# One product for mask and shift, the maxima masked on VectorE, whole-block key copies by two engines in turn: a decode attention kernel on Trainium2

## The chip, the cores and the metric

The kernel runs on one core of a Trainium2 chip. The metric is device microseconds of one execution, the median of several runs. A core has TensorE (matrix products, PE in the profile, its weight loads PEld), VectorE (DVE), ScalarE (ACT), GpSimd (POOL) and SyncE (SP), which issues most of the loads here. Each engine works through its own instructions in their order, and semaphores order the engines among each other.

## The reference

Eight sequences, one new token each, 32 query heads over 8 key heads of width 128, and the last 1024 positions of a cache of 4096. The attention output is gated by a feed-forward network (GEGLU, inner width 1792) of the same normalised input.

```python
def _A_ref(x, k_cache, v_cache, wq, wo):
    W = min(4096, max(256, Sk // 4))
    rep = Hq // Hkv
    q = (x @ wq).reshape(B, Sq, Hq, Dh).transpose(0, 2, 1, 3)
    k = jnp.repeat(k_cache[:, :, Sk - W:, :], rep, axis=1)
    v = jnp.repeat(v_cache[:, :, Sk - W:, :], rep, axis=1)
    scores = jnp.einsum("bhqd,bhkd->bhqk", q, k) * (Dh ** -0.5)
    p = _softmax(scores, axis=-1)
    o = jnp.einsum("bhqk,bhkd->bhqd", p, v)
    return o.transpose(0, 2, 1, 3).reshape(B, Sq, Hq * Dh) @ wo
...
x = A_x
xn = _layernorm(x, axis=-1)
s = _A_ref(xn, A_k_cache, A_v_cache, A_wq, A_wo)
g = _silu((_gelu(xn @ B_w_gate) * (xn @ B_w_up)) @ B_w_down)
return x + s * g
```

## The kernel before

The order of all work is written out by hand: each engine executes in program order. All large loads are issued by SyncE in one queue, into a ring of 16 buffers of 1 MB: first the feed-forward weights, then wq, then key and value blocks in turn, with half a megabyte of wo after every second value block. In all 47.5 MB are read.

At the start TensorE runs fillers (`keep_busy`, line 235: products of ones, 512 columns wide, whose result nobody reads), the layernorm's result is transposed (line 260), and the feed-forward products (lines 274 and 313) and the query products (line 349) follow, with more fillers between them.

The attention is cut into 16 sets (`q`, NQ = 16). A set is one key head and four of the eight sequences (QG = 4); a key block of a set is 4 x 1024 positions. A set has four groups (`g`, `i` = 0 to 3), one 1024-position block each. The positions lie on partitions so that a partition belongs to one of the four sequences, `partition % 4`. The 16 query columns of a set (QC: four sequences, four heads each) are multiplied with every position, so three quarters of the scores belong to the wrong sequence and are masked with -1e30.

- `transposes(g)`: eight TensorE transposes of 128x128 into one PSUM tile `kT_ps` (two such tiles); VectorE copies columns 0 to 639 into `kTa` (line 375), ScalarE the other 384 into `kTb` (line 377).
- `scores(g)`: in the first group of a set, one product of 4 rows (line 386) writes the mask over the whole score tile of 512 columns, and the eight products of line 397 add the scores on it.
- `max_keys(q)`: VectorE's maximum over the columns, per partition (line 408). `max_all(q)`: a TensorE transpose of the maxima (416), VectorE's negated maximum (418), and two diagonal matrices `diag` that hold it in a coarse and a fine part (423, 426), at rows 0 and 32.
- `exponentials(q)`: one product of ones with those rows (line 437, 48 rows) adds the shift to the score tile, then ScalarE's exponential (446) gives `pT`.
- `sums(q)`: eight products of ones with 64 columns of `pT` (451), then VectorE's sum and reciprocal (459, 465).
- `values(g)`: eight products with the value block (476). Each is 64 columns wide (VC = 4 times 16), though only the first 16 accumulate what is used; where fewer than four blocks of columns are left it is 16 wide.
- `normalise(q)` (487), and `project(h)` (502), the product with wo, two heads at a time in the second half of every other set.

The values run two sets behind the scores (LAG = 2). One step of the loop at lines 513 to 535 is, in this order: the transposes of the next group, `max_all` of the set before (step 1), the scores of this group, the sums (step 0) and values of two sets before, the exponentials of the set before (step 2), projections; at the end of a set `normalise`, then `max_keys`. At the end of the program come the last four heads' projections, the gate (541), four transposes (544), the residual (546) and the store.

Of the kernel before, what the change touches and what calls it, by code (L numbers as in the profile page):

```python
# [9 lines left out]
ALU = mybir.AluOpType  # L10
AX = mybir.AxisListType
BF16 = mybir.dt.bfloat16
FP32 = mybir.dt.float32
# [4 lines left out]
def kernel(  # L18
# [33 lines left out]
    nc = tc.nc  # L52
# [6 lines left out]
    W = min(4096, max(256, Sk // 4))  # L59
    win0 = Sk - W  # L60
    F = B_w_gate.shape[1]
    P = nc.NUM_PARTITIONS
    NDC = D // P
    NFC = F // P
    NSC = W // P
# [4 lines left out]
    QG = 4  # L70
    NB = QG
    NCS = QG * NSC
    VC = 4
    AC = 3
    NRING = 16
    MASK = -1.0e30
    NG = Hkv * B
    NQ = NG // QG
    QC = QG * rep
    SH = B // QG  # L80
    LAG = 2

    consts = ctx.enter_context(tc.tile_pool(name="consts", bufs=1))
# [4 lines left out]
    kT_pool = ctx.enter_context(tc.tile_pool(name="kT_pool", bufs=3))  # L88
    p_pool = ctx.enter_context(tc.tile_pool(name="p_pool", bufs=4))
    small = ctx.enter_context(tc.tile_pool(name="small", bufs=2))  # L90
    ps_misc = ctx.enter_context(tc.tile_pool(name="ps_misc", bufs=1, space=PSUM))
# [3 lines left out]
    ps_sum = ctx.enter_context(tc.tile_pool(name="ps_sum", bufs=1, space=PSUM))  # L95
    ps_o = ctx.enter_context(tc.tile_pool(name="ps_o", bufs=1, space=PSUM))
# [75 lines left out]
    for q in range(NQ):  # L172
# [12 lines left out]
        out=ident,  # L185
        in_=ident,
# [8 lines left out]
    ones_pp = consts.tile([P, P], BF16, name="ones_pp")  # L195
    nc.vector.memset(ones_pp, 1.0)

    row_of = consts.tile([QG, P // QG, QG], BF16, name="row_of")
    nc.vector.memset(row_of, 0.0)
    nc.gpsimd.affine_select(  # L200
        out=row_of,
        in_=row_of,
# [6 lines left out]
    other = consts.tile([QG, QG, rep], BF16, name="other")  # L209
    nc.vector.memset(other, MASK)  # L210
    nc.gpsimd.affine_select(
        out=other,
        in_=other,
# [4 lines left out]
        channel_multiplier=-1,  # L218
    )

    LO = 32
    diag = []
    for i in range(2):
        t = consts.tile([LO + QC, QC], BF16, name=f"diag{i}")
        nc.vector.memset(t, 0.0)
        diag.append(t)
    eps_sb = consts.tile([B, 1], FP32, name="eps_sb")
    nc.vector.memset(eps_sb, 1e-5)

# [3 lines left out]
    def keep_busy(n):  # L233
# [12 lines left out]
        out=rstd, in_=mv[:, 1:2], func=ACT.Sqrt, bias=eps_sb, scale=1.0  # L246
# [4 lines left out]
        out=xhat,  # L251
        in0=x_sb,
# [94 lines left out]
    for k in range(NDC):  # L347
        for m in range(Hq):
# [4 lines left out]
                start=(k == 0 and m == 0),  # L353
                stop=(k == NDC - 1),
                skip_group_check=True,
# [5 lines left out]
    kT, sc, pT, mxs, shift, recip = {}, {}, {}, {}, {}, {}  # L361

    def transposes(g):
        q, i = divmod(g, NB)
        kT_ps = ps_kT.tile([P, W], BF16, name="kT_ps")
        for c in range(NSC):
            n = i * NSC + c
            nc.tensor.transpose(  # L368
                kT_ps[:, c * P : (c + 1) * P],
                k_sb[q][:, n * Dh : (n + 1) * Dh],  # L370
                ident,
            )
        own = (NSC - AC) * P
        ta = kT_pool.tile([P, own], BF16, name="kTa")
        nc.vector.tensor_copy(out=ta, in_=kT_ps[:, 0:own])  # L375
        tb = kT_pool.tile([P, W - own], BF16, name="kTb")
        nc.scalar.copy(out=tb, in_=kT_ps[:, own:])  # L377
        kT[g] = [ta[:, c * P : (c + 1) * P] for c in range(NSC - AC)]
        kT[g] += [tb[:, c * P : (c + 1) * P] for c in range(AC)]

    def scores(g):
        q, i = divmod(g, NB)
        hkv, b = divmod(q * QG, B)
        if i == 0:
            sc[q] = ps_sc.tile([P, NCS, QC], FP32, name="sc_ps")
            nc.tensor.matmul(  # L386
                sc[q],
                row_of.rearrange("g e s -> g (e s)"),
                other.rearrange("g s j -> g (s j)")
                .unsqueeze(1)  # L390
                .to_broadcast([QG, NCS, QC]),
                start=True,
                stop=False,
                skip_group_check=True,
            )
        for c in range(NSC):
            nc.tensor.matmul(  # L397
                sc[q][:, i * NSC + c, :],
                kT[g][c],
                qT_all[:, b : b + QG, hkv * rep : (hkv + 1) * rep],  # L400
                start=False,
                stop=False,
                skip_group_check=True,
            )

    def max_keys(q):
        mx = small.tile([P, QC], FP32, name="mx")
        nc.vector.tensor_reduce(  # L408
            out=mx, in_=sc[q].rearrange("p c n -> p n c"), axis=AX.X, op=ALU.max
        )  # L410
        mxs[q] = mx

    def max_all(q):

        mxT_ps = ps_mx.tile([QC, P], FP32, name="mxT_ps")
        nc.tensor.transpose(mxT_ps, mxs[q], ident_f)
        nm = small.tile([QC, 1], FP32, name="nm")
        nc.vector.tensor_reduce(
            out=nm, in_=mxT_ps, axis=AX.X, op=ALU.max, negate=True
        )  # L420
        eye = ident_f[0:QC, 0:QC]
        parts = diag[q % 2]
        nc.vector.tensor_scalar(
            out=parts[0:QC, :], in0=eye, scalar1=nm[:, 0:1], scalar2=None, op0=ALU.mult
        )
        nc.vector.scalar_tensor_tensor(  # L426
            out=parts[LO : LO + QC, :],
            in0=eye,
            scalar=nm[:, 0:1],
            in1=parts[0:QC, :],  # L430
            op0=ALU.mult,
            op1=ALU.subtract,
        )
        shift[q] = parts

    def exponentials(q):
        nc.tensor.matmul(  # L437
            sc[q],
            ones_pp[0 : LO + QC, :],
            shift[q].unsqueeze(1).to_broadcast([LO + QC, NCS, QC]),  # L440
            start=False,
            stop=True,
            skip_group_check=True,
        )
        pT[q] = p_pool.tile([P, NCS, QC], BF16, name="pT")
        nc.scalar.activation(out=pT[q], in_=sc[q], func=ACT.Exp, scale=inv_sqrt_dh)  # L446

    def sums(q):
        sums_ps = ps_sum.tile([P, NB, QC], FP32, name="sums_ps")
        for c in range(NSC):  # L450
            nc.tensor.matmul(  # L451
                sums_ps,
                ones_pp,
                pT[q][:, c * NB : (c + 1) * NB, :],
                start=(c == 0),
                stop=(c == NSC - 1),
            )
        recip[q] = small.tile([P, QC], FP32, name="recip")
        nc.vector.tensor_reduce(
            out=recip[q],  # L460
            in_=sums_ps.rearrange("p c n -> p n c"),
            axis=AX.X,
            op=ALU.add,
        )
        nc.vector.reciprocal(out=recip[q], in_=recip[q])

    o_ps = {}

    def values(g):
        q, i = divmod(g, NB)  # L470
        if i == 0:
            o_ps[q] = ps_o.tile([P, VC, QC], FP32, name="o_ps")
        for c in range(NSC):
            n = i * NSC + c
            wide = VC if n + VC <= NCS else 1
            nc.tensor.matmul(  # L476
                o_ps[q][:, 0:wide, :],
                v_sb[q][:, n * Dh : (n + 1) * Dh],
                pT[q][:, n : n + wide, :],
                start=(n == 0),  # L480
                stop=(n == NCS - 1),
                skip_group_check=True,
            )
# [14 lines left out]
    def project(h):  # L498
        if h == 0:
            sT_ps.append(ps_misc.tile([P, NDC, B], FP32, name="sT_ps", tag="misc"))  # L500
        for d in range(NDC):
            nc.tensor.matmul(  # L502
                sT_ps[0][:, d, :],
                wo_sb[:, h, d * P : (d + 1) * P],
                oT_all[:, h, :],
                start=(h == 0 and d == 0),
                stop=(h == Hq - 1),
                skip_group_check=True,
            )


    transposes(0)
    for q in range(NQ + LAG):
        v = q - LAG
        for i in range(NB):
            g = q * NB + i
            if g + 1 < NG:
                transposes(g + 1)
            if i == 1 and 1 <= q <= NQ:
                max_all(q - 1)  # L520
            if g < NG:
                scores(g)
            if v >= 0:
                if i == 0:
                    sums(v)
                values(v * NB + i)
            if i == 2 and 1 <= q <= NQ:
                exponentials(q - 1)
            if v >= SH and v % SH == 0 and i >= NB // 2:
                for h in range(2):  # L530
                    project((v // SH - 1) * rep + (i - NB // 2) * 2 + h)
        if v >= 0:
            normalise(v)
        if q < NQ:
            max_keys(q)
# [42 lines left out]
```

## Time and profile before

| | us |
|---|---|
| runs of the kernel | 126.57, 126.85, 127.76; median 126.85 |
| the profiled execution | 127.63 |
| its span, first to last instruction | 125.8 |
| TensorE busy | 114.7 (91%) |
| VectorE busy | 64.5 (51%) |
| ScalarE busy | 42.5 (34%) |

The costliest groups that the change touches:

| line, engine | what | times | mean ns |
|---|---|---|---|
| 368 PE | key transposes, 128 columns | 512 | 219 |
| 375 DVE | key copy, 128x640 | 64 | 489 |
| 377 ACT | key copy, 128x384 | 64 | 479 |
| 386 PE | mask product, 4 rows, 512 columns | 16 | 385 |
| 437 PE | shift product, 48 rows, 512 columns | 16 | 386 |
| 451 PE | sums, 64 columns | 128 | 192 |
| 476 PE | values, 64 columns (464) and 16 (48) | 512 | 190 |
| 408 DVE | maxima | 16 | 681 |
| 446 ACT | exponentials, 512 columns | 16 | 601 |

The span runs from the first to the last instruction; the run's own time has 1.83 us around it. TensorE's products are pipelined: the mean of one (219 ns for a transpose) is its way from start to end, while the next starts much sooner, so the distance from start to start is read from the chain of waits or from the timeline. In that chain a row has a start, a duration, an engine, a tile and a line; "issue" is time in which an engine waited for nothing that the profile shows.

### The profile page before, as it was taken

The page shows a single profiled execution, that of the slowest core. Times are in us where ns is not written, and L with a number is a line of the kernel's source. Part 1 is how long each engine was busy: PE and PEld are TensorE (multiplying, and loading weights), DVE is VectorE, ACT ScalarE, POOL GpSimd, SP SyncE. Part 2 cuts the span into 40 slices and gives each one's busy share as a digit, 9 for nine tenths or more (in the row PEclk, how much of TensorE's full clock was granted, in tenths as well). Part 3 has the DMA queues.
Part 4 walks back from the last instruction along what each step waited for, and adds up shares of the span by engine and source line. Part 5 has one row for each costly group of instructions (what it writes and reads, how often), then busy time and mean ns, then how long its engine had stood idle before and what let it go on. Part 6 is the DMA issues. An engine that isn't in the chain of part 4 may idle for free.

```text
span 125.8 us, 4887 instructions
## 1 busy us (share of the span) xinstructions
PE 114.7 (91%) x2197; PEld 89.6 (71%) x2202; DVE 64.5 (51%) x200; ACT 42.5 (34%) x86; POOL 1.2 (1%) x7
## 2 busy tenths in 40 slices
PE   5899999989989999999999898989999999988780
PEld 1366663657777788887888787878787877877570
DVE  5200003010248768756786664858667677765531
ACT  4000005000054644543534254354544435352210
POOL 3000000000000000000000000000000000000000
PEclk9999999999999999999999999999999999999999
DMA  4999999999999999999999999999999999998300
GB/s 89 410 431 417 429 412 417 419 432 427 417 414 398 427 417 417 402 421 435 412 398 431 419 401 424 412 417 412 413 435 410 411 432 411 407 411 357 135 5 3
DMA packets 10325, 47.78 MB, mean 380 GB/s; under 512 B 816, under 2 KB 4928, under 8 KB 5696
## 3 DMA queue, kind: packets, MB, share of 16 engines
q1 hardware_dynamic: 10288, 47.46, 92.5%
q8 instruction: 17, 0.28, 0.9%
q14 instruction: 4, 0.03, 0.1%
q10 hardware_dynamic: 16, 0.01, 0.0%
HBM read 47.46 MB, written 0.01 MB: 377 GB/s over the span
## 4 chain that ended last, share of the span: by engine, by line
PE 73%; DVE 9%; ACT 6%; issue 5%; DMA 4%; ACTq 0%; DVEq 0%
PE kT_ps L368 19%; PE idle_ps L235 12%; PE o_ps L476 10%; PE sc_ps L397 9%; DVE kTa L375 6%; ACT kTb L377 6%; PE gu_ps L274 5%; DMA ring_sb<-in_B_w_gate_dram 4%; PE sc_ps L437 4%; PE sc_ps L386 4%; PE sT_ps L502 3%; PE sums_ps L451 3%; PE qT_ps L349 3%; PE fT_ps L313 1%; DVE mx L408 0%
## 5 line engine op out<-in xcount | busy, mean ns | idle before, releaser
L377 ACT COPY kTb<-kT_ps 128x384 bf16<-128x384 bf16 x64 | 30.6, 479 | 52.6 <-DVE kTa L375 52.6
L375 DVE COPY kTa<-kT_ps 128x640 bf16<-128x640 bf16 x64 | 31.3, 489 | 20.7 <-PE kT_ps L368 20.3
L368 PE MATMUL kT_ps<-ident,ring_sb 128*128 128x128 bf16 x512 | 39.1, 219 | 0.2 <-issue 0.2
L368 PEld LDWEIGHTS <-ring_sb 128*128 128x128 bf16 x512 | 29.4, 97 | 2.4 <-issue 2.2
L476 PE MATMUL o_ps<-pT,ring_sb 128*128 128x64 bf16 (+1 forms) x512 | 25.2, 190 | 2.2 <-issue 2.2
L235 PE MATMUL idle_ps<-ones_w 128*128 128x512 bf16 x53 | 20.0, 521 | 2.2 <-DVE ones_w L181 1.5
L476 PEld LDWEIGHTS <-ring_sb 128*128 128x128 bf16 x512 | 19.1, 97 | 3.0 <-issue 2.8
L397 PE MATMUL sc_ps<-qT_all,kTa 128*128 128x16 bf16 x320 | 17.8, 171 | 0.0
L397 PEld LDWEIGHTS <-kTa 128*128 128x128 bf16 x320 | 14.7, 96 | 4.2 <-issue 2.3
L397 PE MATMUL sc_ps<-qT_all,kTb 128*128 128x16 bf16 x192 | 14.5, 171 | 1.6 <-ACT kTb L377 0.4
L235 PEld LDWEIGHTS <-ones_w 128*128 128x128 bf16 x58 | 6.0, 121 | 8.8 <-issue 6.1
L397 PEld LDWEIGHTS <-kTb 128*128 128x128 bf16 x192 | 9.3, 96 | 3.3 <-ACT kTb L377 1.0
L408 DVE TENSOR_REDUCE mx<-sc_ps 128x16 f32<-128x512 f32 x16 | 10.9, 681 | 0.0
L446 ACT ACTIVATE pT<-sc_ps 128x512 bf16<-128x512 f32 x16 | 9.6, 601 | 2.7 <-PE sc_ps L437 2.6
L274 PEld LDWEIGHTS <-ring_sb 128*128 128x128 bf16 x112 | 7.4, 162 | 2.2 <-issue 1.6
L274 PE MATMUL gu_ps<-xnT_sb,ring_sb 128*128 128x8 bf16 x112 | 7.3, 201 | 0.5 <-DMA ring_sb<-in_B_w_gate_dram 0.5
L291 DVE TENSOR_SCALAR z<-z 128x112 f32<-128x112 f32 x1 | 0.2, 219 | 13.7 <-ACT z L288 13.7
L437 PE MATMUL sc_ps<-diag,ones_pp 48*128 48x512 bf16 x16 | 6.2, 386 | 0.4 <-DVE diag L426 0.4
L451 PE MATMUL sums_ps<-pT,ones_pp 128*128 128x64 bf16 x128 | 6.3, 192 | 0.0
L386 PE MATMUL sc_ps<-other,row_of 4*128 4x512 bf16 x16 | 6.2, 385 | 0.0
L502 PEld LDWEIGHTS <-wo_sb 128*128 128x128 bf16 x128 | 4.3, 96 | 2.5 <-issue 2.5
L502 PE MATMUL sT_ps<-oT_all,wo_sb 128*128 128x8 bf16 x128 | 5.4, 167 | 0.3 <-DVE oT_all L487 0.3
(54 smaller groups left out, 59.4 us busy)
## 6 DMA issues: line engine op xcount, KB each, us to landing
ring_sb<-in_A_k_cache_dram SPq DMA_DIRECT2D x16, 1024.0 KB, 18.8
ring_sb<-in_A_v_cache_dram SPq DMA_DIRECT2D x16, 1024.0 KB, 18.6
ring_sb<-in_A_wq_dram SPq DMA_DIRECT2D x4, 1024.0 KB, 19.5
wo_sb<-in_A_wo_dram SPq DMA_DIRECT2D x8, 512.0 KB, 17.8
ring_sb<-in_B_w_gate_dram SPq DMA_DIRECT2D x2, 896.0 KB, 5.0
ring_sb<-in_B_w_up_dram SPq DMA_DIRECT2D x2, 896.0 KB, 8.4
ring_sb<-in_B_w_down_dram SPq DMA_DIRECT2D x2, 896.0 KB, 12.9
x_sb<-in_A_x_dram ACTq DMA_DIRECT2D x1, 8.0 KB
```

What stands on the lines that cost most here:

```text
L235: nc.tensor.matmul(idle_ps, ones_w[:, 0:P], ones_w, start=True, stop=True)
L274: nc.tensor.matmul(ffn["gu"][:, j, n % 2, :], up_sb[n][:, i, j::NFC], xnT_sb[:, k, :], start=(n == 0 and j == 0 and i == 0), stop=(k == ND ...
L368: nc.tensor.transpose(kT_ps[:, c * P : (c + 1) * P], k_sb[q][:, n * Dh : (n + 1) * Dh], ident,)
L375: nc.vector.tensor_copy(out=ta, in_=kT_ps[:, 0:own])
L377: nc.scalar.copy(out=tb, in_=kT_ps[:, own:])
L386: nc.tensor.matmul(sc[q], row_of.rearrange("g e s -> g (e s)"), other.rearrange("g s j -> g (s j)") .unsqueeze(1) .to_broadcast([QG, NCS, ...
L397: nc.tensor.matmul(sc[q][:, i * NSC + c, :], kT[g][c], qT_all[:, b : b + QG, hkv * rep : (hkv + 1) * rep], start=False, stop=False, skip_g ...
L408: nc.vector.tensor_reduce(out=mx, in_=sc[q].rearrange("p c n -> p n c"), axis=AX.X, op=ALU.max)
L437: nc.tensor.matmul(sc[q], ones_pp[0 : LO + QC, :], shift[q].unsqueeze(1).to_broadcast([LO + QC, NCS, QC]), start=False, stop=True, skip_gr ...
L451: nc.tensor.matmul(sums_ps, ones_pp, pT[q][:, c * NB : (c + 1) * NB, :], start=(c == 0), stop=(c == NSC - 1),)
L476: nc.tensor.matmul(o_ps[q][:, 0:wide, :], v_sb[q][:, n * Dh : (n + 1) * Dh], pT[q][:, n : n + wide, :], start=(n == 0), stop=(n == NCS - 1 ...
L502: nc.tensor.matmul(sT_ps[0][:, d, :], wo_sb[:, h, d * P : (d + 1) * P], oT_all[:, h, :], start=(h == 0 and d == 0), stop=(h == Hq - 1), sk ...
```

## The change

The mask no longer enters the score tile before the scores. The first score product of a set clears the tile, and the scores of the wrong sequences stay in it until the shift product, whose weight `spread` has ones in rows 0 to 63 and the four rows of `row_of` in rows 64 to 67; the rows of `other` stand beside the shift in `diag`, so one product of 68 rows adds shift and mask. The maxima are masked by an addition on VectorE with a tile `mask`, made once at the start by a TensorE product that stands ahead of the first fillers, and a VectorE copy.

A key block is copied whole: by VectorE in even steps, by ScalarE in odd ones. The sums are four products of 128 columns in place of eight of 64. The value products of the last two sets are 128 columns wide in place of 64. In a step of the loop, the sums and values now come before the transpose of the maxima and the scores.

```diff
-    AC = 3
+    SC = 8
+    VCW = 8
...
+    other_ps = ps_misc.tile([P, QC], FP32, name="other_ps", tag="misc")
+    nc.tensor.matmul(
+        other_ps,
+        row_of.rearrange("g e s -> g (e s)"),
+        other.rearrange("g s j -> g (s j)"),
+        start=True,
+        stop=True,
+    )
+    mask = consts.tile([P, QC], FP32, name="mask")
+    nc.vector.tensor_copy(out=mask, in_=other_ps)
...
-    LO = 32
+    LO, MK = 32, 64
     diag = []
     for i in range(2):
-        t = consts.tile([LO + QC, QC], BF16, name=f"diag{i}")
-        nc.vector.memset(t, 0.0)
+        t = consts.tile([MK + QG, QC], BF16, name=f"diag{i}")
+        nc.vector.memset(t[0:MK, :], 0.0)
+        nc.vector.tensor_copy(
+            out=t[MK : MK + QG, :], in_=other.rearrange("g s j -> g (s j)")
+        )
         diag.append(t)
+    spread = consts.tile([MK + QG, P], BF16, name="spread")
+    nc.vector.memset(spread[0:MK, :], 1.0)
+    nc.vector.tensor_copy(
+        out=spread[MK : MK + QG, :], in_=row_of.rearrange("g e s -> g (e s)")
+    )
...
-        own = (NSC - AC) * P
-        ta = kT_pool.tile([P, own], BF16, name="kTa")
-        nc.vector.tensor_copy(out=ta, in_=kT_ps[:, 0:own])
-        tb = kT_pool.tile([P, W - own], BF16, name="kTb")
-        nc.scalar.copy(out=tb, in_=kT_ps[:, own:])
...
+        kT[g] = kT_pool.tile([P, W], BF16, name="kT")
+        if i % 2 == 0:
+            nc.vector.tensor_copy(out=kT[g], in_=kT_ps)
+        else:
+            nc.scalar.copy(out=kT[g], in_=kT_ps)
...
-            nc.tensor.matmul(
-                sc[q],
-                row_of.rearrange("g e s -> g (e s)"),
-                other.rearrange("g s j -> g (s j)")
-                .unsqueeze(1)
-                .to_broadcast([QG, NCS, QC]),
-                start=True,
-                stop=False,
-                skip_group_check=True,
-            )
...
-                start=False,
+                start=(i == 0 and c == 0),
...
-        mxs[q] = mx
+        mxs[q] = small.tile([P, QC], FP32, name="mx_own")
+        nc.vector.tensor_tensor(out=mxs[q], in0=mx, in1=mask, op=ALU.add)
...
-            ones_pp[0 : LO + QC, :],
-            shift[q].unsqueeze(1).to_broadcast([LO + QC, NCS, QC]),
+            spread,
+            shift[q].unsqueeze(1).to_broadcast([MK + QG, NCS, QC]),
...
-        sums_ps = ps_sum.tile([P, NB, QC], FP32, name="sums_ps")
-        for c in range(NSC):
+        sums_ps = ps_sum.tile([P, SC, QC], FP32, name="sums_ps")
+        for c in range(NCS // SC):
...
-            wide = VC if n + VC <= NCS else 1
+            wide = VC if q < NQ - LAG else VCW
+            wide = wide if n + wide <= NCS else 1
...
+            if v >= 0:
+                if i == 0:
+                    sums(v)
+                values(v * NB + i)
             if i == 1 and 1 <= q <= NQ:
                 max_all(q - 1)
             if g < NG:
                 scores(g)
-            if v >= 0:
-                if i == 0:
-                    sums(v)
-                values(v * NB + i)
```

More of the change, by code (lines that the diff above doesn't have):

```diff
@@ L372, in transposes @@
             )
-        own = (NSC - AC) * P
-        ta = kT_pool.tile([P, own], BF16, name="kTa")
-        nc.vector.tensor_copy(out=ta, in_=kT_ps[:, 0:own])
-        tb = kT_pool.tile([P, W - own], BF16, name="kTb")
-        nc.scalar.copy(out=tb, in_=kT_ps[:, own:])
-        kT[g] = [ta[:, c * P : (c + 1) * P] for c in range(NSC - AC)]
-        kT[g] += [tb[:, c * P : (c + 1) * P] for c in range(AC)]
+        kT[g] = kT_pool.tile([P, W], BF16, name="kT")
[3 more added lines that the diff above has]
+            nc.scalar.copy(out=kT[g], in_=kT_ps)
     def scores(g):
@@ L398, in scores @@
                 sc[q][:, i * NSC + c, :],
-                kT[g][c],
+                kT[g][:, c * P : (c + 1) * P],
                 qT_all[:, b : b + QG, hkv * rep : (hkv + 1) * rep],
-                start=False,
+                start=(i == 0 and c == 0),
                 stop=False,
@@ L453, in sums @@
                 ones_pp,
-                pT[q][:, c * NB : (c + 1) * NB, :],
+                pT[q][:, c * SC : (c + 1) * SC, :],
                 start=(c == 0),
-                stop=(c == NSC - 1),
+                stop=(c == NCS // SC - 1),
             )
@@ L471, in values @@
         if i == 0:
-            o_ps[q] = ps_o.tile([P, VC, QC], FP32, name="o_ps")
+            o_ps[q] = ps_o.tile([P, VCW, QC], FP32, name="o_ps")
         for c in range(NSC):
             n = i * NSC + c
-            wide = VC if n + VC <= NCS else 1
+            wide = VC if q < NQ - LAG else VCW
+            wide = wide if n + wide <= NCS else 1
             nc.tensor.matmul(
```

## The prediction

> **What bounds the kernel now.** I read four views, in this order: the slices of the span, the issues of the loads one by one, the chain that ended last, and the first microseconds in order of time.
>
> The slices (DMA busy tenths, then GB/s, 40 slices of 3.14 us):
>
> ```profile
> DMA  4999999999999999999999999999999999998300
> GB/s 89 410 431 417 429 412 417 419 432 427 417 414 398 427 417 417 402 421 435 412 398 431 419 401 424 412 417 412 413 435 410 411 432 411 407 411 357 135 5 3
> ```
>
> Loads run at about 415 GB/s without a hole from 2 us until the last byte, so nothing that the engines do moves the end of the loads. The issues of the last value block and of the last block of wo, each asked for alone, end in microseconds to landing:
>
> ```profile
> ring_sb<-in_A_v_cache_dram SPq DMA_DIRECT2D x1, 1024.0 KB, 17.4
> ```
>
> ```profile
> wo_sb<-in_A_wo_dram SPq DMA_DIRECT2D x1, 512.0 KB, 17.5
> ```
>
> They were issued at 100.72 and 101.94, so they land at 118.1 and 119.4. The same reading puts value blocks 0, 8, 12 and 13 at 37.7, 84.1, 107.0 and 111.9 (issued 17.82, 65.52, 89.50, 93.25; 19.9, 18.6, 17.5, 18.6 to landing). By the timeline the products that read them start at 43.25, 85.72, 107.24 and 112.61. So TensorE runs behind the loads by 5.55, 1.6, 0.2 and 0.75 us: it catches up, and from set 12 on it is all but bound by data. A set of TensorE work takes 4.9 us, or 5.4 with a projection; the loads bring one in 5.6 on average (84.1 to 111.9, five sets). What is gained in the middle is therefore worth nothing by itself; only the last 14 us can move the end.
>
> The chain there (start, us, engine, tile, line):
>
> ```profile
> 111.45 0.47 PE kT_ps L368 x8
> 111.92 0.32 PE sc_ps L386
> 112.24 0.29 PE sc_ps L397 x8
> 112.53 0.25 PE sums_ps L451 x8
> 112.78 0.15 PE o_ps L476 x5
> 112.92 0.56 issue
> ...
> 115.46 0.50 DVE kTa L375
> 116.04 0.49 ACT kTb L377
> ...
> 117.30 0.54 DVE mx L408
> ...
> 120.51 0.92 PE o_ps L476 x32
> ...
> 121.73 0.56 PE sT_ps L502 x16
> ```
>
> Its pitches: eight transposes (128 columns) 0.46, so 58 ns each; eight value or sums products (64 columns) 0.25, 31 ns each; eight scores (16 columns) 0.29, 36 ns; a mask or shift product 0.32. "issue" is a gap of TensorE that no semaphore explains; such gaps of 0.2 to 0.6 come every few microseconds. The two copies of one block run one behind the other (115.46, then 116.04): 1.1 us.
>
> The start:
>
> ```profile
> 1.52 3.60 PE L235 MATMUL idle_ps<-ones_w 128*128 128x512 bf16 x8 [1.52 <-DVE ones_w L181]
> ...
> 2.91 0.21 POOL L211 TENSOR_SCALAR_AFFINE_SELECT other<-other 4x16 bf16<-4x16 bf16 x1
> ...
> 5.05 0.29 PE L260 MATMUL xnT_ps<-ident,xhat 8*128 8x8 bf16 x4
> ```
>
> From the first FFN product at 5.82 to the first key transpose at 33.45, TensorE's own queue is the chain: its operands have all landed long before, and the fillers of line 235 are most of it.
>
> **The change, part by part.**
>
> *Start.* The product for the new mask stands before the fillers in TensorE's queue and needs `other`, ready at 2.91 + 0.21 = 3.12. Everything on TensorE is queued behind it: eight fillers begin at about 3.3 in place of 1.52, and the first FFN product at about 7.6 in place of 5.82: 1.8 us later. On VectorE the mask copy waits for that product (about 3.5), and behind it are six small operations (0.06 to 0.23 each by the memsets of 4x16 and 128x128 and the 128x128 cast, under 1 us in all) and the layernorm chain, which took 1.83 (2.36 to 4.19). It ends near 6.3, under the fillers, which end at 6.9. The 1.8 us passes whole to the first set.
>
> *Steady sets.* The mask product goes: 0.32 per set. The shift product grows from 48 to 68 rows; the 4-row one took 385 ns and the 48-row one 386, so I add nothing (bound: as much again for 20 more rows, 0.02). Sums: 8 x 31 = 0.25 becomes 4 x 58 = 0.23. Net 0.3 per set. The order values before scores changes no count. Copies: VectorE's 128x640 took 489 ns and its 128x32 copy 174, so 0.52 ns a column and 0.69 us for 1024. ScalarE: 384 columns took 479, 512 (the exponentials) 601, 112 (line 288) 265. Slopes of 0.84 to 0.95 give 1.02 to 1.09; in proportion 1.28, at VectorE's slope 0.81. I take 1.05, between the two slopes of its own rows. From the end of a block's transposes to its scores TensorE has a value block, the scores before, the next transposes and another value block to do, 0.25 + 0.29 + 0.46 + 0.25 = 1.25 us, so both copies are covered; without that cover the wait is 1.1 - 1.05, no worse than now. Per set VectorE falls by 4 x 0.49 - 2 x 0.69 - 0.23 = 0.35 us. The added mask addition is priced at 0.23, from the 128x16 product of line 487 (bounds 0.18 to 0.27); before the last set it is hidden, since the transpose of the maxima comes 1.9 us of TensorE work after the last scores. Behind VectorE's 0.69 copy stands the diagonal for the shift product: it was ready 0.34 before its use, 0.2 later still fits.
>
> Before, the lag fell from 5.55 to 0.2 in twelve sets. It now starts at 5.55 + 1.8 and falls by 0.3 x 13 = 3.9 more: TensorE reaches the landings two or three sets earlier, and the late start is recovered. Set 12 is then bound by its landing (107.1).
>
> *The end.* A set with projections now takes 4 x (0.46 + 0.25 + 0.29) + 0.23 for the sums, 0.11 for the transpose of the maxima, 0.32 for the shift product and 0.44 for sixteen projection products (28 ns each): 5.1. So from 107.1 value block 13 starts at 112.2 (landed 111.9). Adding pitches from there: scores 60 end at 112.74; transposes, values, maxima (0.11) and scores of the next step 113.85; the last transposes issue from 113.85 and end with their tail of 0.61 at 114.46; ScalarE's copy runs 114.5 to 115.55; the last scores, which TensorE reaches at 115.42, go from 115.6 to 115.96. Before, they ended at 116.80, and the maxima waited further for the normalising behind the values, to 117.16. The new order has the values first, so the maxima start at 115.98: 1.18 earlier. What cost that time before was 0.56 of "issue" and the queue of diagonal, copy, copy.
>
> Against it: the mask addition, 0.25 with its hand-over. Two blocks of wide values (8 x 58) now stand before the transpose of the maxima: 0.07 of wait. Most of all the last set's 32 value products: 25 of them are now 128 columns wide, 25 x 58 + 7 x 31 = 1.67 against 0.92 in the chain, 0.75 more. Other wide products of the last two sets lie in TensorE's waits. Sum: -1.18 + 0.25 + 0.07 + 0.75 = -0.11. My walk has no "issue" gap in 12 us where the old one had one of 0.56 on the chain; part of them falls in waits, so I add 0.2: span 125.9.
>
> [...] Five fillers took 2.15 us at 15.20 and 1.10 at 29.18: TensorE ran at half speed until about 23, after the one unbroken run of fillers (19.20, 3.62 us).
> [...]
>
> **How it stands to the runs.** The profiled execution took 127.63 for a span of 125.8 (1.83 outside); the median is 126.85, 0.78 less. Span 125.9 + 1.83 - 0.78 = 126.95; I say 126.9.
>
> **Rivals.**
> *The late start is not recovered.* If a wait takes the place of the mask product (scores waiting for ScalarE's copy, the shift product for VectorE's, or copies that still run one behind the other), the saving per set vanishes. It decides below 1.8 - 0.2 over 13 sets, about 0.13 us a set. Then value block 12 starts near 109, and the end is 1.8 later with the tail's -0.1: 128.6. For it: the diagonal has only 0.14 to spare. Against: TensorE's pitches add to the whole of the set from 85.28 to 90.69.
> *Half speed until the sets.* Some 26 fillers after 23 us at 0.43 in place of 0.22 add 5.5 to the 1.8: 5.55 + 7.3 against 5.3 + 3.9 of catching up leaves 3.6, so about 130.
> *Faster.* If the wide products run at 31 ns, -0.75, and no gap falls on the chain, -0.2, and the first wait of the last scores goes, -0.16, it is 125.8 (126.9 - 1.11); with one more gap of 0.3 gone, 125.5. The landing at 118.1 would allow 124.7.
>
> **Chances.** No change to speak of 0.57 (its own range 126.0 to 127.8); late start kept 0.20; half speed 0.05; faster 0.15; the rest, 0.03, on the slow side. About 1% is what can be told from no change. Faster 0.15, same 0.57, slower 0.28. The range 125.5 to 128.6 leaves out half speed, half of the late start and the end of the fast case.
>
> **What would show it.** First FFN product near 7.6; no line 386; ScalarE's copies near 1.05 and VectorE's near 0.69; value products starting within 0.3 of the landings from set 10 on; the last scores near 116.0; the last 32 value products about 1.8 long; projection near 121.6. If value block 12 starts over 1 us after its landing, the second case holds; if the fillers still take 0.43 after 30 us, the third; if the last value products take 1.1, the fast one.

## The result, and the profile after

| | kernel before | changed kernel |
|---|---|---|
| median of 10 runs, us | 126.98 (126.28 to 128.83) | 128.40 (128.10 to 128.87) |
| ratio, 95% interval | | 1.0104 (1.0072 to 1.0137) |
| profiled execution, its span, us | 127.63, 125.8 | 128.33, 126.6 |
| first FFN product, first key transposes | 5.82, 33.45 | 7.34, 35.11 |
| value blocks 12 and 13 land | 107.0, 111.9 | 107.7, 113.1 |
| their products start | 107.29, 112.61 | 107.79, 113.17 |
| last value and last wo block land | 118.1, 119.4 | 119.5, 120.9 |
| last projection starts | 121.73 | 122.48 |

The changed kernel is 1.0% slower, or 1.4 us. The medians here and below count all executions; the ratios leave out those over 1.5% above the fastest of their kernel. The time lies in the range of the prediction (125.5 to 128.6), 1.5 above its likeliest 126.9. Two lines of the table hold the surprise: the loads, which the prediction took as fixed, land later, the last by 1.5 us.

The start and the catching-up went as forecast. The chain of the changed kernel at its start (start, us, engine, tile, line):

```profile
3.16 0.17 PE other_ps L223
3.33 3.53 PE idle_ps L256 x8
...
7.34 1.79 PE gu_ps L295 x28
...
35.28 0.46 PE kT_ps L389 x8
```

The mask product waits for its operand until 3.16, and the fillers behind it start 1.7 late; 1.66 of that is left at the first transposes. Later, in order of time (the bracket says how long TensorE stood idle, and for what):

```profile
107.79 0.41 PE L487 MATMUL o_ps<-pT,ring_sb 128*128 128x64 bf16 x8 [0.77 <-DMA ring_sb<-in_A_v_cache_dram]
...
113.17 0.41 PE L487 MATMUL o_ps<-pT,ring_sb 128*128 128x64 bf16 x8 [0.46 <-DMA ring_sb<-in_A_v_cache_dram]
...
116.84 0.38 PE L461 MATMUL sums_ps<-pT,ones_pp 128*128 128x128 bf16 x4 [0.16 <-ACT pT L456]
...
117.44 0.17 DVE L421 TENSOR_TENSOR mx_own<-mx,mask 128x16 f32<-128x16 f32 x1
...
118.00 0.27 PE L426 MATMUL mxT_ps<-ident_f,mx_own 128*16 128x128 f32 x1
...
120.44 1.72 PE L487 MATMUL o_ps<-pT,ring_sb 128*128 128x128 bf16 x32
...
122.48 0.54 PE L513 MATMUL sT_ps<-oT_all,wo_sb 128*128 128x8 bf16 x16 [0.32 <-DVE oT_all L498]
```

TensorE now waits for the value blocks; from set 8 to set 13 each starts 0.05 us after its landing, where the kernel before was 0.2 to 1.7 behind. Then come the two costs of the wide products: the masked maxima are ready at 117.61, but their transpose stands behind sixteen of them until 118.00, and the last 32 take 1.72. The copies and the shift product, on the page (busy, mean ns after the bar), behind the busy tenths of the DMA engines and the loads' queue (packets, MB, share of 16 engines' span):

```profile
DMA  4999999999999999999999999999999999999400
...
q1 hardware_dynamic: 10288, 47.46, 93.0%
...
L398 ACT COPY kT<-kT_ps 128x1024 bf16<-128x1024 bf16 x32 | 32.4, 1012 | 48.3 <-PE kT_ps L389 48.3
...
L396 DVE COPY kT<-kT_ps 128x1024 bf16<-128x1024 bf16 x32 | 22.1, 691 | 27.0 <-PE kT_ps L389 26.8
...
L447 PE MATMUL sc_ps<-diag,spread 68*128 68x512 bf16 x16 | 6.0, 376 | 2.3 <-DVE diag L436 0.4
```

The same 10288 packets (most of them one row of a load: 8 KB of a key or value block, 1 KB of wo) and 47.46 MB took 92.5% of 125.8 us before, 116.4 us, and 93.0% of 126.6 now, 117.7. The engines of the queue are busy without a hole until the end, so the loads are not held back by late issues: their own packets take 1.3 us more. The issue of the last wo block, at 102.78:

```profile
wo_sb<-in_A_wo_dram SPq DMA_DIRECT2D x1, 512.0 KB, 18.1
```

### The profile page after: what moved, and what is told of

The parts are those of the page before. It is cut to its first block, busy times and chain, and to the rows that moved or that the text cites. A ratio compares the mean times of both kernels' runs of the same rounds, so it can differ in the third digit from the quotient of the medians.

```text
span 126.6 us, 4687 instructions
## 1 busy us (share of the span) xinstructions
PE 107.5 (85%) x2123; PEld 87.8 (69%) x2123; DVE 60.1 (47%) x189; ACT 44.5 (35%) x54; POOL 1.2 (1%) x7
## 3 DMA queue, kind: packets, MB, share of 16 engines
q1 hardware_dynamic: 10288, 47.46, 93.0%
HBM read 47.46 MB, written 0.01 MB: 375 GB/s over the span
## 4 chain that ended last, share of the span: by engine, by line
PE 47%; DMA 30%; DVE 13%; issue 4%; ACT 3%; POOLq 0%; POOL 0%; DVEq 0%
PE idle_ps L256 15%; DMA ring_sb<-in_A_v_cache_dram 15%; DMA ring_sb<-in_A_k_cache_dram 15%; PE kT_ps L389 9%; DVE kT L396 5%; PE gu_ps L295 5%; PE o_ps L487 5%; PE sc_ps L406 3%; PE qT_ps L370 3%; PE sc_ps L447 2%; ACT kT L398 2%; DVE mx L417 1%; PE sums_ps L461 1%; DVE diag L436 1%; DVE diag L433 1%
## 5 line engine op out<-in xcount | busy, mean ns | idle before, releaser
L398 ACT COPY kT<-kT_ps 128x1024 bf16<-128x1024 bf16 x32 | 32.4, 1012 | 48.3 <-PE kT_ps L389 48.3
L396 DVE COPY kT<-kT_ps 128x1024 bf16<-128x1024 bf16 x32 | 22.1, 691 | 27.0 <-PE kT_ps L389 26.8
L389 PEld LDWEIGHTS <-ring_sb 128*128 128x128 bf16 x512 | 29.5, 97 | 6.5 <-DMA ring_sb<-in_A_k_cache_dram 4.1
L487 PE MATMUL o_ps<-pT,ring_sb 128*128 128x64 bf16 (+2 forms) x512 | 25.6, 193 | 3.2 <-DMA ring_sb<-in_A_v_cache_dram 3.0
L487 PEld LDWEIGHTS <-ring_sb 128*128 128x128 bf16 x512 | 21.7, 98 | 4.7 <-DMA ring_sb<-in_A_v_cache_dram 4.2
L406 PE MATMUL sc_ps<-qT_all,kT 128*128 128x16 bf16 x512 | 22.6, 170 | 2.6 <-issue 1.7
L256 PE MATMUL idle_ps<-ones_w 128*128 128x512 bf16 x58 | 21.6, 520 | 0.0
L406 PEld LDWEIGHTS <-kT 128*128 128x128 bf16 x512 | 18.8, 96 | 4.0 <-issue 1.9
L295 PEld LDWEIGHTS <-ring_sb 128*128 128x128 bf16 x112 | 7.5, 159 | 1.8 <-issue 1.8
L447 PE MATMUL sc_ps<-diag,spread 68*128 68x512 bf16 x16 | 6.0, 376 | 2.3 <-DVE diag L436 0.4
L461 PE MATMUL sums_ps<-pT,ones_pp 128*128 128x128 bf16 x64 | 6.2, 219 | 0.2 <-ACT pT L456 0.2
L426 PE MATMUL mxT_ps<-ident_f,mx_own 128*16 128x128 f32 x16 | 4.4, 274 | 0.7 <-DVE kT L396 0.7
L370 PEld LDWEIGHTS <-ring_sb 128*128 128x128 bf16 x128 | 3.8, 96 | 1.4 <-issue 0.6
```

The lines of the kernel that those rows point to most:

```text
L256: nc.tensor.matmul(idle_ps, ones_w[:, 0:P], ones_w, start=True, stop=True)
L295: nc.tensor.matmul(ffn["gu"][:, j, n % 2, :], up_sb[n][:, i, j::NFC], xnT_sb[:, k, :], start=(n == 0 and j == 0 and i == 0), stop=(k == ND ...
L370: nc.tensor.matmul(qT_ps[:, m, :], q_sb[k][:, m * Dh : (m + 1) * Dh], xnT_sb[:, k, :], start=(k == 0 and m == 0), stop=(k == NDC - 1), ski ...
L389: nc.tensor.transpose(kT_ps[:, c * P : (c + 1) * P], k_sb[q][:, n * Dh : (n + 1) * Dh], ident,)
L396: nc.vector.tensor_copy(out=kT[g], in_=kT_ps)
L398: nc.scalar.copy(out=kT[g], in_=kT_ps)
```

## The experiments

**Theory and rivals.** The two kernels load the same bytes in the same order. But the changed one has two more constants, `mask` (64 bytes in each partition) and `spread` (256), and all tiles behind them lie 320 bytes further: in the memory map of the built programs wo starts at byte 18944 of each partition before, a multiple of 512, and at 19264 after, remainder 320; the ring's remainder of 512 goes from 320 to 128. The place theory says that this makes the packets longer. Contention says that engines which read a block as soon as it lands get into the way of the loads behind it. Chance says that the two profiles differ as any two do. Runs sent together shared a chip and the runs of the kernel before; the median of those moved between 126.98 and 127.84 from one comparison to the next (126.28 to 129.16 over all of them), while most variants of the changed kernel scatter by less than a microsecond. So variants are compared with each other where they can be.

**The kernel before, moved by 320 bytes.**

```diff
+    pad = consts.tile([P, 160], BF16, name="pad")
     eps_sb = consts.tile([B, 1], FP32, name="eps_sb")
```

> The kernel before, with 320 unused bytes per partition among the constants, so that wo, the ring and all behind them lie where the changed kernel has them (the mask and spread tiles moved them by 320). Nothing is computed otherwise. Place theory: the loads are slower because of where their targets lie; blocks of wo take 1.4 us in place of 1.27, the last load lands near 120.7 in place of 119.4, and the time is about 1% above the kernel before. Rival, contention: the loads are slower because engines now read blocks as soon as they land; then this kernel takes what the kernel before takes, within 0.3%, and its last load lands near 119.4. Rival, chance: the same as contention here.

Measured: 128.43, ratio to the kernel before 1.0059 (1.0017 to 1.0100). Its queue line and the last wo block's issue, at 102.74:

```profile
q1 hardware_dynamic: 10288, 47.46, 93.0%
```

```profile
wo_sb<-in_A_wo_dram SPq DMA_DIRECT2D x1, 512.0 KB, 18.2
```

93.0% of a span of 126.4 is 117.6 us of packets, and the last load lands at 120.9: the changed kernel's numbers, with the work of the kernel before. The time is 0.6% longer and not the 1% that was forecast, and its interval reaches down to 0.2%, which the contention theory would allow; it is the landing, 1.5 later, that rules contention out.

**The changed kernel, moved on to the old remainders.**

```diff
+    pad = consts.tile([P, 96], BF16, name="pad")
     eps_sb = consts.tile([B, 1], FP32, name="eps_sb")
```

> The changed kernel with 192 more unused bytes among the constants, so that wo starts again at a multiple of 512 bytes and the ring at the same remainder of 512 (320) as before. Place theory: blocks of wo take 1.27 us again, the last load lands 1.2 to 1.5 earlier than in the changed kernel (near 119.5), and the time falls by about 1.3 us, to near 127.1. Contention or chance: no change against the changed kernel, 128.4.

Measured: 126.86 (126.58 to 127.42), 1.5 below the changed kernel, ratio to before 0.9956 (0.9924 to 0.9987). Its queue line, then TensorE's rows at the end:

```profile
q1 hardware_dynamic: 10288, 47.46, 92.7%
```

```profile
111.96 0.41 PE L488 MATMUL o_ps<-pT,ring_sb 128*128 128x64 bf16 x8
...
116.74 0.27 PE L427 MATMUL mxT_ps<-ident_f,mx_own 128*16 128x128 f32 x1
...
119.19 1.72 PE L488 MATMUL o_ps<-pT,ring_sb 128*128 128x128 bf16 x32
...
121.22 0.54 PE L514 MATMUL sT_ps<-oT_all,wo_sb 128*128 128x8 bf16 x16 [0.32 <-DVE oT_all L499]
```

92.7% of 125.3 is 116.2 us, and value block 13 lands at 111.9 as in the kernel before. The projection starts at 121.22, 1.26 earlier than in the changed kernel and 0.5 earlier than before. The place theory holds both ways.

**The kernel before again, in a second profile.**

> The kernel before, unchanged, in a second profile. If chance had made the loads of the first one quick, the last load would land elsewhere than near 119.4 and the 1 KB packets would not take 46 ns; by the place theory both repeat, and what differs is how far TensorE runs behind the loads.

Measured: 126.53 in one execution, 93.2% of 124.7, 116.2 us; the 1 KB packets take 46.6 ns, the last load lands at 119.1. Chance is out too. What differs is the start:

```profile
7.39 1.10 PE idle_ps L235 x5
...
10.11 2.15 PE idle_ps L235 x5
...
32.40 0.46 PE kT_ps L368 x8
```

By the timeline the first key transposes begin at 32.24 and not at 33.45, and value block 13 starts 0.4 behind its landing, not 0.75.

**Which place.** wo at a multiple of 512 with the ring at the changed kernel's remainder, then both at multiples of 512 (with narrow products):

```diff
+    pad = consts.tile([P, 96], BF16, name="pad")
     eps_sb = consts.tile([B, 1], FP32, name="eps_sb")
...
     gT_sb = persist.tile([P, NDC, B], FP32, name="gT_sb")
+    pad2 = persist.tile([P, 160], BF16, name="pad2")
```

> The changed kernel with 192 unused bytes ahead of wo and 320 behind it: wo starts at a multiple of 512 as before, the ring has the changed kernel's remainder of 512 (128). If the place of wo is all, its 1 KB packets take 46 ns again and the time is that of the padded kernel, 126.9. If the ring's place counts too, the 8 KB packets stay at 316 ns in place of 313: 16 engines with 288 of them each, 0.9 us, and the time falls only by some 0.7, to 127.7.

Measured: 126.54 (126.38 to 126.89); 92.8% of 124.8, 115.8 us; the last load lands at 118.7. The first case of the expectation holds. In the trace's packet records the 1 KB packets take 46.6 ns on the mean (before 46.4, changed 48.8) and the 8 KB packets 311.9 (313.0, 316.0). So the ring's remainder of 512 is not what made its packets long: with the same 128 they take 311.9 here and 316.0 in the changed kernel. What did shows when the records are sorted by time. Ahead of the first row of wo, at 40 us, the 8 KB packets take 314.1 ns in this kernel and in the changed one (314.4 before); behind it 311.1 here, 316.7 in the changed kernel and 312.5 before. Those within 0.3 us of a 1 KB packet take 312.1, 319.3 and 312.5. So the misplaced rows of wo hold up the packets beside them too; how they do it stays open.

> The changed kernel with wo and the ring both at multiples of 512 bytes, and narrow value products. If a multiple of 512 is what helps, the 8 KB packets fall below 313 ns (the ring had remainder 320 before) and the last load lands before 119.4; the time would fall to or below that of the kernel with the old remainders and narrow products. If only the place of wo matters, both take the same time.

Measured: 124.88 (124.81 to 125.12), ratio to before 0.9826 (0.9779 to 0.9872), the fastest kernel of this study. Its queue line and, from its chain, the end:

```profile
q1 hardware_dynamic: 10288, 47.46, 93.5%
```

```profile
118.07 0.92 PE o_ps L489 x32
118.99 0.02 issue
119.01 0.24 DVE oT_all L500
119.25 0.04 issue
119.29 0.56 PE sT_ps L515 x16
```

93.5% of 123.4 is 115.4 us, the 8 KB packets take 310.4 ns, the last load lands at 118.4, and the time is 0.90 below that of the same kernel with the old remainders (125.78, below), on the same chip.

Ahead of the first row of wo, the 8 KB packets take 309.8 to 310.2 ns where the ring starts at a multiple of 512, and 313.5 to 314.8 at remainders 320 and 128. The loads of these runs read the same rows and only their targets moved. Why the place of a target changes the time of its packets, no run here shows, and no other remainders were run.

**Narrow value products to the end.** In the changed kernel, then with the old remainders as well:

```diff
-    VCW = 8
+    VCW = 4
```

> The changed kernel with the value products of the last two sets 64 columns wide again. The tail is TensorE's: the last 32 value products take 1.07 in place of 1.72 and the time falls by 0.65 to about 127.8. Rival: the end hangs on the last load (wo, landed 120.9), so that less than 0.65 comes through; since the projection starts at 122.5 it should not. A second rival, that the wide products hold the clock up: then the projection and what follows get slower and the gain is below 0.3.

Measured: 127.04 (126.85 to 127.24), 1.36 below the changed kernel, twice what was expected. TensorE's rows at the end:

```profile
116.71 0.64 PE L487 MATMUL o_ps<-pT,ring_sb 128*128 128x64 bf16 x16
117.28 0.28 PE L426 MATMUL mxT_ps<-ident_f,mx_own 128*16 128x128 f32 x1
...
119.73 1.07 PE L487 MATMUL o_ps<-pT,ring_sb 128*128 128x64 bf16 x32
121.11 0.54 PE L513 MATMUL sT_ps<-oT_all,wo_sb 128*128 128x8 bf16 x16 [0.32 <-DVE oT_all L498]
```

The last 32 products give 1.72 - 1.07 = 0.65. The sixteen ahead of the maxima's transpose give another 0.3 to 0.4: it starts 0.05 after the maxima are ready (117.23) and not 0.39. The remaining 0.4 is no gain of the edit that this run can show: the loads of this profile came 0.4 earlier (value block 13 at 112.73, the last wo at 120.5), which the edit doesn't explain. Against the changed kernel with the late mask, on the same chip, the gain is 1.09. The projection that follows takes the same 0.54 as behind the wide products of the changed kernel, so the second rival is out.

> The changed kernel with both undone: 192 unused bytes, so that wo and the ring have their old remainders of 512, and 64-column value products to the end. The place gives 1.5 us (128.4 to 126.9 in the run with the padding alone), the narrow products give at least 0.65. If the two add, 126.2; if the landing of the last wo block (119.4) stops it, the projection cannot start before 119.5, which allows 1.7 below the padded kernel, so it should not stop it. Rival: narrow products gave 1.4 in their own run, which would be 125.5; then there is more to them than the last 32.

Measured: 125.78 (125.73 to 125.97), ratio to before 0.9907 (0.9866 to 0.9947). Against the padded kernel with wide products 1.08. The two edits nearly add (1.54 + 1.36 = 2.90; 128.40 - 125.78 = 2.62; the chips differ). With the loads as before and without the wide products, what is left of the change makes the kernel 0.9% faster.

**The mask made later.**

```diff
-    nc.tensor.matmul(
-        other_ps,
...
     nc.vector.tensor_copy(out=qT_all, in_=qT_ps.rearrange("p h b -> p b h"))
+    nc.tensor.matmul(
+        other_ps,
...
```

> The changed kernel with the product and the copy that make the mask moved behind the query products, so that the fillers start at 1.5 again and the first FFN product at 5.8. If the late start is recovered by set 8, as the trace of the changed kernel says, the time stays at 128.4 within 0.3. If the start were the cause of the loss, it would fall by 1.4 to 1.8.

Measured: 128.13 (127.73 to 128.89), 0.27 below the changed kernel. The fillers start at 1.5 again, the first FFN product only at 6.47, since VectorE's preparations still stand ahead of the layernorm. Value blocks 8 to 13 start 0.05 after their landings, as in the changed kernel. The run is a weak test of the late start: by the first key transposes only 0.36 of the earlier start is left (34.76 against 35.11). That the late start is recovered rests on those landings, and on the executions that are sorted by their clock under "A late start in the kernel before".

> The fastest variant with the mask made after the query products. The start is recovered either way, so 124.9 within 0.2. If it is faster by more, the late start still costs something.

Measured: 125.18 against the 124.88 of the same kernel with the early mask, on another chip: no gain. Its profile can't be compared: in that execution, of 166.4 us, TensorE ran at half speed (sixteen transposes in 1.82 us; see the last section).

**A late start in the kernel before.**

```diff
-    keep_busy(8)
+    keep_busy(12)
```

> The kernel before with four more fillers at the start (4 x 0.43 = 1.7 us), about the late start that the change brings, and nothing else. Its TensorE is still 0.3 to 0.8 us behind the loads at sets 12 and 13, so what is lost at the start should come out at the end: 1.0 to 1.7 above the kernel before. If the late start is recovered without the removal of the mask products, no change.

Measured: 127.80, ratio 1.0039 (0.9999 to 1.0080): about a third of what was expected, and not clear of nothing. The profiled execution started later by less than was planned. Its chain:

```profile
1.52 4.47 PE idle_ps L235 x12
6.49 1.79 PE gu_ps L274 x28
8.27 1.90 PE idle_ps L235 x5
```

Twelve fillers at 0.43 are 5.2 us; these took 4.47, so some of them ran at the 0.22 of full speed: about three, as an estimate from the 0.69 that is missing and 0.21 for each. The first key transposes began at 33.26: as early as in the first profile of the kernel before, but 1.02 later than in the second, which also has a stretch of full speed at the start (five fillers in 1.10 from 7.39 on). The last projection starts 0.43 later than there (121.06 against 120.63).

What a late start costs the kernel before can be read from its own executions, by the mean granted clock that was recorded with each. The five profiles of this study whose fillers ran at full speed (0.22 each) for a while before 11 us read 0.94 to 0.95; the seven whose fillers took 0.43 each until about 20 us read 0.99 or 1.00. (Two fit neither group: the late-mask kernel reads 0.925, and the execution of 166.4 us at half speed reads 1.00.) Of the executions that the ratios count, the kernel before has medians of 126.55 to 126.84 on the three chips where the clock reads below 0.95, and of 127.47 to 127.90 where it reads 0.97 or more. Its two profiles are one of each: 0.944, transposes from 32.24, 126.53; and 0.999, transposes from 33.45, 127.63. So a start about 1.2 later goes with 0.8 to 1.1 more at the end. With twelve fillers every execution reads below 0.95; of those that the ratio counts the median is 127.41, 0.6 above the kernel before in that group on the same chip (126.81). The changed kernel doesn't part like this: 126.89 and 126.70 with 192 bytes of padding, 127.12 and 127.05 with narrow products, though the transposes of its profiles start anywhere from 33.89 (0.946) to 35.32 (1.00). This fits the prediction: the changed kernel recovers a late start, the kernel before does so only in part. It is a comparison of executions as they came, since no run here changes the clock alone.

**The kernel before in the place of the fastest.** 512 bytes ahead of wo and 192 ahead of the ring:

```diff
+    pad = consts.tile([P, 256], BF16, name="pad")
     eps_sb = consts.tile([B, 1], FP32, name="eps_sb")
...
     gT_sb = persist.tile([P, NDC, B], FP32, name="gT_sb")
+    pad2 = persist.tile([P, 96], BF16, name="pad2")
```

> The kernel before with 512 and 192 unused bytes, so that wo and the ring lie exactly where the fastest variant so far has them. If the place alone makes that variant fast, this takes its 124.9. If the change itself helps once the place is equal, this lies above it: loads end 0.5 to 0.7 earlier than in the kernel before, TensorE is 0.3 to 0.8 behind the loads at set 13 and has its old last sets, so 126 to 126.5, and it scatters as the kernel before does.

Measured: 126.24 (125.53 to 128.12), ratio to before 0.9919 (0.9877 to 0.9960), against 0.9826 (0.9779 to 0.9872) for the changed kernel with narrow products in the same place. The last load lands at 118.6. So the place is worth about 0.8% to the kernel before, and the change without its wide products about 0.9% on top; the first has some 0.4% of doubt, the second some 0.6%.

**The old order of scores and values, in the fastest variant.**

```diff
-            if v >= 0:
-                if i == 0:
-                    sums(v)
-                values(v * NB + i)
             if i == 1 and 1 <= q <= NQ:
                 max_all(q - 1)
             if g < NG:
                 scores(g)
+            if v >= 0:
+                if i == 0:
+                    sums(v)
+                values(v * NB + i)
```

> The fastest variant (narrow products, wo and ring at multiples of 512) with the scores before the sums and values again, as in the kernel before. The maxima of the last set then wait for the normalising behind the last values of the set, as before (0.2 to 0.4 later), and a value block that has not landed no longer holds the scores back. By the reading of the end in the prediction the new order is worth 0.2 to 0.4, so 125.1 to 125.3; if holding the scores back costs as much, no change; if it costs more, it is faster than 124.9.

Measured: 125.22 (124.91 to 125.38), ratio 0.9859 (0.9823 to 0.9894). The direction is the expected one, but the intervals overlap and the chips differ. In the two profiles value block 13 starts at the same time (110.95 and 110.96) and the projection at 119.38 against 119.29. The order is worth 0.1 by the profiles and 0.3 by the medians, and neither is clear of noise.

## Why the prediction was right or wrong

**The step that failed is the first one:** "nothing that the engines do moves the end of the loads", and with it the landings of 118.1 and 119.4 that the walk of the end was built on. The work of the engines indeed did not move it (the last load lands at 120.9 in the changed kernel and in the kernel before with 320 bytes of padding), but the change did, by two constants that push the targets of the loads 320 bytes on. It was priced at nothing because nothing in the diff touches a load. It measured 1.5 us: 128.40 against 126.86 with 192 bytes of padding (1.3 in the profiled spans, 126.6 against 125.3, and against the late-mask kernel on the same chip, 128.13). That the time lies in the stated range all the same is luck: the range reaches to 128.6 for the sake of the late-start rival, and that is not what happened.

**The rest of the sum held, its total in part by luck.** With the loads where they were, the kernel takes 126.86; the prediction was 126.9. Two errors cancel there. The walk gave a span of 125.9, and the padded kernel has 125.3. And the walk took off 0.78 to get from the profiled execution to the median, where the padded kernel needs only 0.20 (127.06 to 126.86). The 0.78 belonged to the kernel before, whose first profile was one of its late-starting executions. In the changed kernel itself it is about 0 (128.33 and 128.40), so of the 1.45 that the prediction missed by, 0.7 lies in the span (126.6 for 125.9) and the other 0.7 in this step. Point by point:

- The late start: 1.8 forecast, 1.5 at the first FFN product and 1.66 at the first transposes.
- Its recovery: forecast two or three sets ahead of set 12; from set 8 on each value block starts 0.05 after landing. The late-start rival, whose 128.6 is near the measured time, is therefore not what happened: its sign, a value block 12 over 1 us behind, is absent. (The prediction read the start of block 12 before as 107.24; the timeline has 107.29, which changes nothing.)
- Durations: 691 ns for VectorE's copy (690 forecast), 1012 for ScalarE's (1050), 376 for the product of 68 rows (386), 175 for the mask addition (230).
- The end: from value block 13 to the maxima of the last set 3.78 forecast (112.2 to 115.98), 3.55 measured (113.17 to 116.72). Before it was 4.55.
- The wide products: 0.75 + 0.07 forecast. In the profiles 0.65 for the last 32 and 0.39 for the wait of the maxima's transpose, in the runs 1.1 to 1.4 in all. The mechanism was right; the second term was too small. Of its 0.39, 0.16 is a wait of the sums, ahead of the two value blocks, for the exponentials, which the walk didn't have; the rest was not traced further.
- Half speed until the sets did not happen in the changed kernel: five fillers took 1.10 us from 28.97 on.

**Why the sum came out near nothing, and the time did not.** The change takes TensorE work away in the middle, where TensorE then waits for loads (3.0 us for value blocks and 2.4 for key blocks over the span); at the end it gains about 1 us before the last maxima and gives all of it back to the wide products and the mask addition (from the last maxima to the last projection 5.76, before 4.57). Left over was the place of the loads' targets.

## What to carry to other kernels

Here two constant tiles, 320 bytes of each partition together, cost 1.5 us (128.40 against 126.86), and both targets at multiples of 512 bytes gained 0.9 (124.88 against 125.78). So where loads bound a kernel, look where a constant tile pushes the targets of the loads, compare the packets' time (share of the queue times the span) of two profiles before reading anything else into them, and try the large targets on multiples of 512 bytes. Work taken off TensorE, which then waited for the value blocks from set 8 on, moved only the part behind the last value block that it waited for (block 13, to the last maxima: 3.55 us in place of 4.55).

## What the runs showed of the hardware that was not expected

The place of a load's target: the same loads took 115.3 to 115.5 us of packets with wo and the ring at multiples of 512 bytes, 116.1 to 116.4 with wo there and the ring at remainder 320, 115.8 with wo there and the ring at 128, and 117.5 to 117.8 with wo at 320 and the ring at 128, whichever kernel ran (four, five, one and four profiles).

TensorE's clock: in the second profile of the kernel before, five fillers took 1.10 us at 7.39 and 2.15 again at 10.11, so full speed came after the first fillers and went again; in the first profile it came only at 23 us, though the mean granted clock of that one reads 0.999 and of the second 0.944. The time of a filler, 0.43 or 0.22, is the surer sign; what brings full speed, no run here shows. And the profiled execution of the variant with multiples of 512 and the late mask did not reach it in the sets: sixteen transposes took 1.82 us at 40.85, where they take 0.9 otherwise, the last 32 value products 2.03 at 158.11 in place of 1.07, and the execution took 166.4 us in place of 125.2.
